# Moving the SBUF tiles of an attention and two-MoE kernel to multiples of 512 bytes

## The chip, the cores and the metric

The kernel runs on one NeuronCore of a Trainium2 chip, in one launch. The metric is device time in microseconds (us). Before the change, three runs gave a median of 1016.65 us (1014.98 to 1017.88). Lower is better.

## What is computed

Causal attention with a decay bias on 4 batches, 8 heads, 576 positions and head size 64, then two feed-forward stages on the 2304 tokens of width 512. All inputs and outputs are float32. The reference, cut to what matters:

```
scores = q @ k.T / sqrt(64)
cum    = cumsum(maximum(s, 0));  bias = minimum(-(cum[i] - cum[j]), 0)
attn   = softmax(where(causal, -1e9, scores + bias));  x = attn @ v   # -> [2304, 512]
x      = ((x @ w_a) * (x @ w_b)) @ w_out            # d_ff 1536
h      = x @ w_in                                    # d_ff 2048
out    = (maximum(h,0) + alpha*minimum(h,0)) @ w_out2
```

## The kernel before, in words

**Blocks.** The 2304 tokens are cut into four blocks of 512 and one of 256 (`blocks`). For each block `ffn(blk)` runs both feed-forward stages, and while it does, the attention steps of the next block are put between its matmuls (`steps`). Before the first block, `first_attention` does what block 0 needs.

**Float32 by three passes.** A float32 product is made of three matmuls on float32r operands. Each operand is split into a rounded part and a rest: x into `xh` and `xl`, a weight tile into `wh` and `wl` (`parts`), an activation g into `gh` and `gl` (`split_g`). `mm3` (lines 1076 to 1080) then issues three matmuls, L1077 to L1079; the second GEMM of the second stage issues its own three, L1188 to L1190:

```
nc.tensor.matmul(o, wh, ih, start=first, stop=False)   # L1077
nc.tensor.matmul(o, wh, il, start=False, stop=False)   # L1078
nc.tensor.matmul(o, wl, ih, start=False, stop=last)    # L1079
```

The second argument is the stationary operand (128 columns, loaded into the array before each matmul), the third the moving one, streamed past it: 512 columns in blocks 0 to 3, 256 in block 4. In the trace a matmul is written `bank<-moving,stationary`, so `bank<-xh,wh` streams `xh`, and `bank<-wh,gh` (L1188) streams `wh`, always 512 columns.

**Steps of a block.** Stage one has 12 steps (1536/128). A step is two times `into` (4 slices of x, three matmuls each: 24 that stream x) and four slices of the way back (12 that stream `gh` or `gl`). Stage two has 16 steps (2048/128). A step is one `into` (12 that stream x) and the way back, 12 matmuls that stream `wh` or `wl` (6 in the last block).

**Weights.** In block 0 each weight tile comes from `w64` as 64-bit words into a `raw` tile (`first`, a DMA on SP's queue), is decoded by ACT and DVE into `w32`, split into `wh` and `wl`, and also stored to DRAM (`store`, a DMA on ACT's queue, `w_d<-w`). In blocks 1 to 4 pairs of tiles come back from there into the same `raw` tiles (`load_pair`).

**Order.** The planner class `Order` fixes, from estimated durations, the order of all instructions while the kernel is built; at run time each engine works through its list and waits on semaphores.

**Where tiles lie.** Each tile pool takes one stretch of SBUF, one after the other in the order in which the pools are opened (lines 224 to 233). An address here is the byte within each partition. Before the change `alpha_sb` (64 bytes) stands among the constants, so that everything behind it starts at 64 modulo 512; the five `raw` tiles (4104 bytes, laid at steps of 4128) stand ahead of the weights and activations, so that these start at 480 modulo 512.

Of the kernel before, what the change touches and what calls it, by code (L numbers as in the profile page):

```python
# [9 lines left out]
F32 = mybir.dt.float32  # L10
F32R = mybir.dt.float32r
I32 = mybir.dt.int32
# [9 lines left out]
P = 128  # L22
# [26 lines left out]
def f32(ap):  # L49
    return ap.bitcast(F32)  # L50
# [148 lines left out]
def attention_two_moe_kernel(  # L199
# [15 lines left out]
    NF2 = alpha.shape[1]  # L215
    NW = w64.shape[0]
    NF1 = (NW - 2 * NF2) // 3
    WN = 512
# [5 lines left out]
    const = ctx.enter_context(tc.tile_pool(name="const", bufs=1))  # L224
    xp = ctx.enter_context(tc.tile_pool(name="xp", bufs=1))
    dram = ctx.enter_context(tc.tile_pool(name="dram", bufs=1, space=DRAM))
    raw = ctx.enter_context(tc.tile_pool(name="raw", bufs=1))
    work = ctx.enter_context(tc.tile_pool(name="work", bufs=1))
    small = ctx.enter_context(tc.tile_pool(name="small", bufs=12))
    wraw = ctx.enter_context(tc.tile_pool(name="wraw", bufs=1))  # L230
    wsp = ctx.enter_context(tc.tile_pool(name="wsp", bufs=6))
    gp = ctx.enter_context(tc.tile_pool(name="gp", bufs=3))
    ft = ctx.enter_context(tc.tile_pool(name="ft", bufs=4))
    ps = ctx.enter_context(tc.tile_pool(name="ps", bufs=1, space=PSUM))
    W32, RAW, KQ, VB, CB, KL, TOPS = 4, 5, 3, 4, 3, 2, 2
    ZT = 3
# [55 lines left out]
    def dma(o, i):  # L292
        yield {"sp": 480}, 700
        nc.sync.dma_start(o, i)
        yield {"dma": prod(o.shape) / (180 if o.dtype == U16 else 90)}, 900

    def split(src, hi, lo, sbuf=True):
        yield from copy(hi, src, 0.52 if sbuf else 1.04)
        yield from sub(lo, src, f32(hi), sbuf)
# [9 lines left out]

    ident = const.tile([P, P], F32, name="ident")  # L310
    make_identity(nc, ident)
    alpha_sb = const.tile([P, NF2], F32, name="alpha_sb")

    banks = [ps.tile([P, 512], F32, name=f"bank{i}") for i in range(8)]
    ab, acc = banks[2:4], banks[4:8]
# [665 lines left out]
    def decode(n, r, w):  # L981

        top = tops[n % TOPS]
        yield of_top
        yield {"act": 90 + 1.2 * WN}, SEEN
        nc.scalar.activation(
            top.bitcast(F16).rearrange("p (n t) -> p n t", t=2)[:, :, 1],
            r.bitcast(BF16)[:, 4:4 + 4 * WN].rearrange("p (n t) -> p n t", t=4)[:, :, 0],
            AF.Copy, scale=0.5,
        )  # L990
        rest = r[:, 0:2 * WN].rearrange("p (n t) -> p n t", t=2)[:, :, 1]
        yield from dve(
            WN, 1.04, nc.vector.scalar_tensor_tensor, w, rest, 13, top,
            op0=ALU.logical_shift_right, op1=ALU.bitwise_or, port=True
        )
        run.give(of_top, run.t)

    def load_pair(i):
        yield of_raw
        r = wraw.tile([P, 2 * WN + 2], F32, name="raw", tag="raw", bufs=RAW)  # L1000
        w = r[:, 0:2 * WN].rearrange("p (c n) -> p c n", c=2)
        pairs[i, "w"] = w
        yield from dma(w, w_d[i:i + 2].rearrange("c p n -> p c n"))

    def load_w(n):

        i = n % NW
        got = []

        def acquire():  # L1010

            if n:
                yield turns[n - 1]
            yield fetched
            yield of_w

        def first():
            yield of_raw
            r = wraw.tile([P, 2 * WN + 2], I32, name="raw", tag="raw", bufs=RAW)
            yield from dma(r.bitcast(U16)[:, 1:1 + 4 * WN], w64[i].bitcast(U16))  # L1020
            yield of_w32
            w = wraw.tile([P, WN], I32, name="w32", tag="w32", bufs=W32)
            if n == NW - 1:
                for j in range(2):
                    run.give(of_stack, run.t)
            source.append(w)
            yield from decode(n, r, w)
            run.give(of_raw, run.t)

        def again():  # L1030
            if i % 2 == 0:
                pairs[i] = run.spawn(load_pair(i))
            yield pairs[i - i % 2]
            source.append(pairs[i - i % 2, "w"][:, i % 2, :])

        def parts():
            yield turns[n]
            h = wsp.tile([P, WN], F32R, name="wh", tag="wh")
            l = wsp.tile([P, WN], F32R, name="wl", tag="wl")
            got.extend((h, l))  # L1040
            yield from split(f32(source[0]) if n < NW else source[0], h, l)
            if n < NW:
                run.spawn(keep(stored), run.t)
            elif i % 2:
                run.give(of_raw, run.t)

        def store():
            yield fetched
            yield {"act": 330}, 700
            nc.scalar.dma_start(w_d[i].bitcast(I32), source[0])  # L1050
            yield {"dma": P * WN / 90}, 900

        def keep(stored):
            yield stored
            run.give(of_w32, run.t)

        source = []
        fetched = run.spawn(first() if n < NW else again(), slack=SL_LOAD)
        stored = run.spawn(store()) if n < NW else None
        turns[n] = run.spawn(acquire())  # L1060
        return got, run.spawn(parts(), slack=SL_PARTS)
# [227 lines left out]
```

## Time and profile before

| | |
|---|---|
| median of three runs | 1016.65 us |
| profiled execution | 1019.79 us, span from first to last instruction 1018.0 us |
| mean granted TensorE clock | 0.995 |
| TensorE (PE) busy | 997.0 us, 98% of the span |
| VectorE (DVE), ScalarE (ACT), GpSimd (POOL) busy | 683.3, 554.9 and 241.6 us |
| DMA | 208.85 MB, mean 205 GB/s |

The profile covers one execution. Its timeline gives the start of each instruction. A matmul's duration in it is modelled, about 0.4 us for 512 columns, and overlaps the next one's, so the rate of TensorE is read from start to start: the time from one matmul's start to the next one's. The view by stretches counts the instructions that touch a stretch, gives the granted clock there, and the share of time for which the 16 DMA engines moved packets.

### The profile page before, as it was taken

To read this page: it belongs to the slowest core of one execution; us is meant where nothing else is said; L and a number is where in the kernel's file an instruction comes from. 1 tells how busy PE (TensorE), PEld (TensorE's weight loads), DVE (VectorE), ACT (ScalarE), POOL (GpSimd) and SP (SyncE) were. 2 spreads that over 40 slices of the span, in tenths; PEclk is the share of its full clock that TensorE was granted. 3 is DMA by queue.
4 is the path that set the end of the run, shared out by engine and by line. 5 is a ranking of instruction groups with operands and counts; after the bars stand their busy time and mean duration, and the time that the engine had idled before them with its cause. 6 is when DMAs were issued, how large, how long until landed. Compare 5 with 4: busy or idle time off the path is not lost.

```text
span 1018.0 us, 16223 instructions
## 1 busy us (share of the span) xinstructions
PE 997.0 (98%) x5381; PEld 810.5 (80%) x5381; DVE 683.3 (67%) x1590; ACT 554.9 (55%) x1133; POOL 241.6 (24%) x307
## 2 busy tenths in 40 slices
PE   6999999998999999999999999999999999999998
PEld 5667777776888888788888888888888888889997
DVE  6887767895578676866478677954444465546685
ACT  5865656775565455655454446544433354446574
POOL 2121112321232243433133124422010022220032
PEclk9999999998999999999999999999999999999999
DMA  6699999999677858458287656554542424317551
GB/s 164 206 282 347 354 329 335 322 335 308 231 258 220 243 167 257 144 166 259 83 265 238 201 201 181 179 176 129 182 144 88 156 86 135 109 63 248 181 174 60
DMA packets 149156, 208.85 MB, mean 205 GB/s; under 512 B 36112, under 2 KB 80144, under 8 KB 149072
## 3 DMA queue, kind: packets, MB, share of 16 engines
q1 hardware_dynamic: 139280, 189.99, 59.5%
q10 hardware_dynamic: 9792, 17.83, 4.7%
q8 instruction: 42, 0.69, 0.3%
q14 instruction: 42, 0.34, 0.1%
HBM read 164.18 MB, written 43.59 MB: 204 GB/s over the span
## 4 chain that ended last, share of the span: by engine, by line
PE 92%; DMA 4%; DVE 3%; ACT 0%; issue 0%; SPq 0%; POOL 0%; ACTq 0%; DVEq 0%; POOLq 0%
PE bank L1077 21%; PE bank L1078 21%; PE bank L1079 21%; PE bank L1188 6%; PE bank L1189 6%; PE bank L1190 6%; PE bank L765 3%; PE bank L501 2%; PE bank L527 2%; DMA cb<-cum_d 2%; PE bank L705 1%; PE bank L826 1%; DMA raw<-in_w_dram 1%; DVE z L277 1%; DMA kq<-in_kq_a_dram 1%; PE bank L517 1%
## 5 line engine op out<-in xcount | busy, mean ns | idle before, releaser
L1077 PE MATMUL bank<-xh,wh 128*128 128x512 f32 (+1 forms) x800 | 301.5, 377 | 2.1 <-DVE g L277 2.1
L1079 PE MATMUL bank<-xh,wl 128*128 128x512 f32 (+1 forms) x800 | 299.2, 374 | 0.0
L1078 PE MATMUL bank<-xl,wh 128*128 128x512 f32 (+1 forms) x800 | 298.5, 373 | 0.0
L269 ACT ACTIVATE wh<-raw 128x512 fp32r<-128x512 f32 x268 | 167.6, 628 | 102.5 <-PE bank L1078 60.6
L283 DVE TENSOR_TENSOR wl<-raw,wh 128x512 fp32r<-128x512 f32 x188 | 130.8, 698 | 100.3 <-ACT wh L269 94.5
L283 POOL TENSOR_TENSOR wl<-raw,wh 128x512 fp32r<-128x512 f32 x84 | 110.0, 1310 | 342.9 <-ACT wh L269 329.4
L1077 PEld LDWEIGHTS bank<-xh,wh 128*128 128x128 f32 x800 | 150.8, 189 | 35.8 <-issue 4.6
L1079 PEld LDWEIGHTS bank<-xh,wl 128*128 128x128 f32 x800 | 150.4, 188 | 28.9
L1078 PEld LDWEIGHTS bank<-xl,wh 128*128 128x128 f32 x800 | 150.3, 188 | 28.8
L269 ACT ACTIVATE gh<-g 128x512 fp32r<-128x512 f32 (+1 forms) x140 | 82.3, 588 | 70.7 <-DVE g L277 67.9
L1188 PE MATMUL bank<-wh,gh 128*128 128x512 f32 x288 | 115.2, 400 | 2.9 <-ACT wh L269 2.9
L283 DVE TENSOR_TENSOR gl<-g,gh 128x512 fp32r<-128x512 f32 (+1 forms) x128 | 87.9, 687 | 42.0 <-ACT gh L269 40.2
L1189 PE MATMUL bank<-wl,gh 128*128 128x512 f32 x288 | 114.3, 397 | 0.0
L1190 PE MATMUL bank<-wh,gl 128*128 128x512 f32 x288 | 113.3, 394 | 0.0
L261 ACT ACTIVATE z<-z,mn 128x128 f32<-128x128 f32 (+4 forms) x144 | 82.9, 577 | 52.8 <-DVE mn L277 52.8
L1077 PE MATMUL bank<-gh,wh 128*128 128x512 f32 (+1 forms) x240 | 90.1, 375 | 0.0
L1078 PE MATMUL bank<-gl,wh 128*128 128x512 f32 (+1 forms) x240 | 89.4, 372 | 0.2 <-DVE gl L283 0.2
L1079 PE MATMUL bank<-gh,wl 128*128 128x512 f32 (+1 forms) x240 | 88.7, 370 | 0.0
L261 ACT ACTIVATE m<-bank 128x512 f32<-128x512 f32 (+1 forms) x80 | 44.2, 553 | 81.1 <-PE bank L1079 80.7
L288 DVE TENSOR_SCALAR m<-m,alpha_sb 128x512 f32<-128x512 f32 (+1 forms) x68 | 33.2, 489 | 63.2 <-ACT m L261 62.2
L269 ACT ACTIVATE a_sb<-bank 128x512 f32<-128x512 f32 (+1 forms) x60 | 33.0, 550 | 66.5 <-PE bank L1079 64.0
L1188 PEld LDWEIGHTS bank<-wh,gh 128*128 128x128 f32 x288 | 54.6, 189 | 17.1 <-ACT wh L269 3.4
(91 smaller groups left out, 1369.6 us busy)
## 6 DMA issues: line engine op xcount, KB each, us to landing
raw<-w_d SPq DMA_DIRECT2D x136, 512.0 KB, 4.1
raw<-in_w_dram SPq DMA_DIRECT2D x68, 512.0 KB, 6.1
w_d<-w ACTq DMA_DIRECT2D x68, 256.0 KB, 5.6
zd<-zt SPq DMA_DIRECT2D x48, 192.0 KB, 4.1
pt<-zd SPq DMA_DIRECT2D x48, 192.0 KB, 4.0
kq<-in_kq_a_dram SPq DMA_DIRECT2D x16, 512.0 KB, 5.1
vb<-in_v_dram SPq DMA_DIRECT2D x112, 64.0 KB, 4.0
zd<-zt SPq DMA_DIRECT2D x24, 256.0 KB, 2.7
```

What stands on the lines that cost most here:

```text
L261: nc.scalar.activation(o, i, func, **k)
L269: nc.scalar.activation(o, i, AF.Copy, scale=by)
L283: (nc.gpsimd if eng == "pool" else nc.vector).tensor_tensor(o, i0, i1, op=ALU.subtract)
L288: (nc.gpsimd if eng == "pool" else nc.vector).tensor_scalar(o, i, s0, s1, op0=ALU.mult, op1=ALU.mult)
L501: nc.tensor.matmul(d, qs[:, r * P:n], k[:, 0:n], start=i == 0, stop=i == 1)
L765: nc.tensor.matmul(pv[64 * j:64 * j + 64, r * P:(r + 1) * P], got[0][:, c, j * D:(j + 1) * D], p[:, :, r * (r + 1) // 2 + c, :], start=c = ...
L1077: nc.tensor.matmul(o, wh, ih, start=first, stop=False)
L1078: nc.tensor.matmul(o, wh, il, start=False, stop=False)
L1079: nc.tensor.matmul(o, wl, ih, start=False, stop=last)
L1188: nc.tensor.matmul(acc[t], gh[:, c], wh, start=first, stop=False)
L1189: nc.tensor.matmul(acc[t], gh[:, c], wl, start=False, stop=False)
L1190: nc.tensor.matmul(acc[t], gl[:, c], wh, start=False, stop=last)
```

## The change

Two pools move. `small` (the minima and sums of the softmax, 32 bytes apart) goes behind the large tiles and also takes `alpha_sb`; the `raw` tiles leave the pool `wraw` for a new pool `w64p`, the last one.

```
-    small = ctx.enter_context(tc.tile_pool(name="small", bufs=12))
     wraw = ctx.enter_context(tc.tile_pool(name="wraw", bufs=1))
     wsp = ctx.enter_context(tc.tile_pool(name="wsp", bufs=6))
     gp = ctx.enter_context(tc.tile_pool(name="gp", bufs=3))
     ft = ctx.enter_context(tc.tile_pool(name="ft", bufs=4))
+    small = ctx.enter_context(tc.tile_pool(name="small", bufs=12))
+    w64p = ctx.enter_context(tc.tile_pool(name="w64p", bufs=1))
...
-    alpha_sb = const.tile([P, NF2], F32, name="alpha_sb")
+    alpha_sb = small.tile([P, NF2], F32, name="alpha_sb", bufs=1)
...
-        r = wraw.tile([P, 2 * WN + 2], F32, name="raw", tag="raw", bufs=RAW)
+        r = w64p.tile([P, 2 * WN + 2], F32, name="raw", tag="raw", bufs=RAW)
...
-            r = wraw.tile([P, 2 * WN + 2], I32, name="raw", tag="raw", bufs=RAW)
+            r = w64p.tile([P, 2 * WN + 2], I32, name="raw", tag="raw", bufs=RAW)
```

In the built programs every engine has the same instructions in the same order, with the same waits; only the addresses differ:

| tile | first address before (modulo 512) | after (modulo 512) |
|---|---|---|
| `xh`, `xl`: 4 slices of 2048 bytes each | 20544 (64) | 20480 (0) |
| `pt`, `kq`, `vb`, `z`, `zt`, `kl` | 59456 for the first (64) | 59392 (0) |
| `cb1`, second buffer | 108864 (320) | 108800 (256) |
| `w32`, also `kh` and `qs` | 176096 (480) | 154624 (0) |
| `wh`, `wl` | 184288 (480) | 162816 (0) |
| `gh`, `gl` | 208864 (480) | 187392 (0) |
| `a_sb`, `m`, `g`, `o` | 221152 (480) | 199680 (0) |
| the five `raw` tiles | 155456 (320, 352, 384, 416, 448) | 208704 (320, 352, 384, 416, 448) |

The `raw` tiles keep their places modulo 512, one by one.

## Rows read from the trace of the kernel before

**Rows 1.** Page, part 1: engine, busy us, share of the span, instructions.

```profile
PE 997.0 (98%) x5381; PEld 810.5 (80%) x5381; DVE 683.3 (67%) x1590; ACT 554.9 (55%) x1133; POOL 241.6 (24%) x307
```

**Rows 2.** Page, part 4: the chain that ended last, by engine and by line.

```profile
PE 92%; DMA 4%; DVE 3%; ACT 0%; issue 0%; SPq 0%; POOL 0%; ACTq 0%; DVEq 0%; POOLq 0%
PE bank L1077 21%; PE bank L1078 21%; PE bank L1079 21%; PE bank L1188 6%; PE bank L1189 6%; PE bank L1190 6%; PE bank L765 3%; PE bank L501 2%; PE bank L527 2%; DMA cb<-cum_d 2%; PE bank L705 1%; PE bank L826 1%; DMA raw<-in_w_dram 1%; DVE z L277 1%; DMA kq<-in_kq_a_dram 1%; PE bank L517 1%
```

**Rows 3.** Waits of TensorE: total us, times, longest; first and last of nine.

```profile
PE bank L366 <- DVE cum L355: 5.7, 1, 5.7
...
PE bank L1078 <- DVE gl L283: 0.2, 1, 0.2
```

**Rows 4.** TensorE groups by line and shape: count, busy us, mean ns.

```profile
L1077 PE MATMUL bank<-xh,wh 128*128 128x512 f32 x640 | 256.4, 401 | 2.1 <-DVE g L277 2.1
...
L1188 PE MATMUL bank<-wh,gh 128*128 128x512 f32 x288 | 115.2, 400 | 2.9 <-ACT wh L269 2.9
...
L1077 PE MATMUL bank<-gh,wh 128*128 128x512 f32 x192 | 76.5, 399 | 0.0
```

**Rows 5.** Timeline of TensorE, x streaming: start us, modelled us, instruction.

```profile
737.16 0.39 PE L1077 MATMUL bank<-xh,wh 128*128 128x512 f32 x1
737.39 0.39 PE L1078 MATMUL bank<-xl,wh 128*128 128x512 f32 x1
737.62 0.40 PE L1079 MATMUL bank<-xh,wl 128*128 128x512 f32 x1
737.86 0.39 PE L1077 MATMUL bank<-xh,wh 128*128 128x512 f32 x1
```

**Rows 6.** Timeline of TensorE, wh and wl streaming.

```profile
717.63 0.39 PE L1188 MATMUL bank<-wh,gh 128*128 128x512 f32 x1
717.85 0.39 PE L1189 MATMUL bank<-wl,gh 128*128 128x512 f32 x1
718.08 0.39 PE L1190 MATMUL bank<-wh,gl 128*128 128x512 f32 x1
718.31 0.39 PE L1188 MATMUL bank<-wh,gh 128*128 128x512 f32 x1
```

**Rows 7.** Stretches, TensorE alone: us, busy (instructions touched), clock, DMA share, GB/s.

```profile
733.64:742.01 8.37, 8.37 (x37) 1.00 0.43 140
694.41:699.98 5.57, 5.57 (x25) 1.00 0.33 97
...
954.12:957.00 2.88, 2.88 (x26) 1.00 0.73 194
```

**Rows 8.** Timeline of TensorE, L521, which streams one repeated column.

```profile
29.39 0.33 PE L521 MATMUL bank<-rows,cums 64*128 64x384 f32 x2
29.55 0.48 PE L527 MATMUL bank<-kq 64*128 64x384 f32 x2
...
30.43 0.38 PE L521 MATMUL bank<-rows,cums 64*128 64x512 f32 x2
30.65 1.02 PE L527 MATMUL bank<-kq 64*128 64x512 f32 x4
```

**Rows 9.** Timeline of TensorE in a stretch of half clock.

```profile
250.43 0.63 PE L1188 MATMUL bank<-wh,gh 128*128 128x512 f32 x1
...
251.71 0.63 PE L1188 MATMUL bank<-wh,gh 128*128 128x512 f32 x1
```

**Rows 10.** Stretches, all engines: PE, PEld, DVE, ACT, POOL; clock, DMA share, GB/s.

```profile
50.00:250.00 200.00, 194.93 (x1025) 149.42 (x1025) 151.25 (x361) 128.23 (x255) 42.03 (x55) 0.99 1.00 327
250.00:490.00 240.00, 237.88 (x1268) 193.77 (x1267) 172.10 (x393) 129.25 (x267) 75.83 (x96) 0.99 0.69 214
```

**Rows 11.** ScalarE groups by line and shape: count, busy us, mean ns.

```profile
L269 ACT ACTIVATE wh<-raw 128x512 fp32r<-128x512 f32 x268 | 167.6, 628 | 102.5 <-PE bank L1078 60.6 <-PE bank L1190 17.1 <-issue 16.7
...
L269 ACT ACTIVATE kh<-kq 128x512 fp32r<-128x512 f32 x16 | 9.3, 619 | 3.9 <-DMA kq<-in_kq_a_dram 2.0 <-PE bank L501 1.9
```

**Rows 12.** DMA queue of ACT (w_d<-w): packets, MB, share of 16 engines.

```profile
q10 hardware_dynamic: 9792, 17.83, 4.7%
```

## Prediction

> **What bounds the kernel now.** I read the page's busy times first: TensorE is busy for 997.0 of 1018.0 us [rows 1]. The chain of waits says the same, 92% of it TensorE, and two thirds of that the three lines of `mm3` [rows 2]. TensorE's nine waits start at 5.7 us for the longest and end at 0.2; two thirds of what they sum to lies before block 0 [rows 3]. So nothing is gained here by ending a wait sooner, only by a matmul that takes less, and a layout can change only that: no instruction, no order and no wait differs.
>
> How long a matmul takes is read from start to start. Three matmuls that stream x follow each other in 737.86 - 737.16 = 0.70 us, 233 ns each [rows 5]; three that stream `wh` and `wl` in 718.31 - 717.63 = 0.68 us, 227 ns each [rows 6]. 512 columns at 2.4 GHz are 213.3 ns, so there are 13 to 20 ns in every matmul that are no column. Three more rows say what they are not. At the low clock, 1.2 GHz, three of the same matmuls start in 1.28 us, 427 ns each, which is 512 columns and nothing else [rows 9]: a fixed price for changing the stationary operand would be there too. L521 is also float32r and also changes its stationary operand each time, but it streams one column over and over, so that hardly anything is fetched; the next line starts 0.22 us after it for 512 columns and 0.16 for 384 [rows 8], which, at the 10 ns that these rows resolve, is the columns and a few ns at most. And the two kinds with the extra time differ from each other: x lies at 64 modulo 512 and takes 233, `wh` at 480 and takes 227. All three point to the fetch of the moving operand from SBUF at the high clock, and to its address.
>
> The sizes fit a simple picture. 227 ns are 544 column times, and 544 = 17 x 32: a run of 2048 bytes that starts between multiples of 128 bytes touches 17 pieces of 128 bytes, where 16 would hold it. In block 4, 24 matmuls of 256 columns take 2.88 us, 120 ns each [rows 7], or 288 column times = 9 x 32, where 8 pieces would do. If the fetch runs at just the rate of the columns, one piece per 32 columns, the piece too many is what the extra time is. That is argued from sums, not shown; no operand at a multiple of 128 bytes is streamed at this rate in the trace.
>
> **The change part by part.** What TensorE spends in the two feed-forward stages, from rows: a step of stage one is 24 + 12 matmuls in 8.37 us, a step of stage two 12 + 12 in 5.57 us [rows 7]. Four blocks of 12 and 16 steps make 4 x (12 x 8.37 + 16 x 5.57) = 758 us. Block 4 adds 12 x 36 x 0.120 + 16 x (12 x 0.120 + 6 x 0.23) = 97 us. Together 855 us, 84% of the span, in 3 x (640 + 192 + 288) = 3360 matmuls of 512 columns [rows 4] and 624 of 256.
>
> Moving x, weights and activations to 0 modulo 512. The trace shows no such operand, so the price is bounded from both sides. Lower end: the start to start of L521, taken as the columns and 2.5 ns, since 0.22 and 0.16 both allow that: 216 ns for 512 columns and 109 for 256. The steps become 36 x 0.216 = 7.78 and 24 x 0.216 = 5.18 us, the four blocks 4 x (12 x 7.78 + 16 x 5.18) = 705 us, block 4 12 x 36 x 0.109 + 16 x (12 x 0.109 + 6 x 0.216) = 89 us: 61 us less. Upper end: all at the 233 ns of rows 5, steps of 8.40 and 5.60 us, 4 us more. I take the lower end, because the two sizes of the extra time are each just one 128-byte piece, and because the stationary and the moving operand then have the same place modulo 512, as only the 227 ns kind has now.
>
> Block 0 won't give all of its share. Its quarter of the 53 us that the four blocks save is 13 us, but from 50 to 250 us the 16 DMA engines are busy for 1.00 of the time at 327 GB/s [rows 10], with the weights coming in and going out. What TensorE saves there it will mostly wait for the next weight tile. I keep 3 of 13 us: 10 less saved. After block 0 the share is 0.69, DVE is busy for 172 of 240 us and ACT for 129 [rows 10]; a pace 6% faster leaves both under 80%. For waits that are hidden now and come out there (splits of g, transposed probabilities) I take off 2 us; none to 10 is the range.
>
> Everything else is about nothing. ACT's copies of 512 columns take 628 ns from `raw` tiles and 619 from `kq`, which lie at five and at one place modulo 512 [rows 11]; so an ACT instruction may change by 2% at most, 11 us of ACT's 555, hidden behind TensorE; without that cover it would be these 11 us. The `raw` loads keep their places modulo 512. The stores `w_d<-w` now start at a multiple of 512; they are 4.7% of the DMA engines' time, 48 us, in block 0 [rows 12], and a tenth either way would be 5 us there, in the stage that the DMAs set. I take nothing and keep 5 us each way for the range.
>
> Sum: -61 + 10 + 2 = -49 us. On the profiled execution (span 1018.0 us and 1.8 around it, 1019.8) that is 971; it ran 3 us above the median of the three runs, 1016.65, on which I forecast 1016.65 - 49 = **968 us**.
>
> **Rivals.** *Only the worse of the two places is mended.* The 13 ns are a start-up of the fetch, not a piece too many, and only the 6 ns between x and `wh` go, with the 50 ns by which a step of stage one, 8.37 us, is longer than 24 x 0.2333 + 12 x 0.2267 = 8.32. Then all run at 226.7: steps of 8.16 and 5.44 us, 4 x (12 x 0.21 + 16 x 0.13) = 18 us less, of which block 0 gives back 3: 1001 us. For it: the extra is 13 ns for 256 columns and for 512 alike, as a start-up would be. Against it: L521 and the half clock show none.
>
> *The layout doesn't matter.* x differs from `wh` and `gh` also in its PSUM banks (2 and 3 against 4 to 7) and in where in SBUF it lies; if one of these makes the 6 ns, the time stays 1017 us. For it: no row holds all else equal. Against it: L521 also ends in a bank and has no extra. [...]
>
> *Slower: the same start for everything collides.* Moving and stationary operand are both fetched, and now begin at the same place modulo 512, on a multiple of 64 as x does already; x at 64 is the slower kind, `wh` at 480 the faster. If a start on such a multiple is what costs, x stays at 233 and the 1440 matmuls that stream weights and activations go from about 230 ns ((8.37 - 24 x 0.2335)/12) to 233: with the steps of 8.40 and 5.60 us above, 4 x (12 x 0.03 + 16 x 0.03) and as much per matmul in block 4, 3.7 us more, 1020 us. It decides the sign if these 1440 lose 2 ns or more each, 3 us, while x stays.
>
> **How the numbers follow.** Fetch without the extra piece, 968: 0.43. Only the worse place mended, 1001: 0.25. Between these two (a part of the extra, 975 to 998): 0.06. No effect, 1017: 0.13. Slower, 1020 and up: 0.13. A measurement of this kernel tells about 0.3% (3 us) from no change. Faster is then 0.43 + 0.25 + 0.06 = 0.74, the same 0.13, slower 0.13. The likeliest case's own range is 955 (all 61 us) to 980 (10 more us of new waits, DMAs 2 worse). The range of 8 in 10 has to hold both faster cases and about half of no effect: 955 to 1017.
>
> **What would show it.** In the profile after, a step of stage one should take 7.8 us instead of 8.37 and one of stage two 5.2 instead of 5.57, at clock 1.00; x and weights should have the same start to start, 216 ns, and block 4's 256 columns 109. TensorE's busy share should fall in block 0 alone, with waits on `wh` or `wl` and the DMA share still near 1.00; ACT's 628 ns should stay. If steps take 8.16 and 5.44 the first rival is right; if x keeps 233 ns, the address is not what sets it and the forecast is wrong.

## The result and the profile after

The changed kernel took 1005.9 us (median of 4 runs, 1001.92 to 1007.81) against 1017.26 us for the kernel before beside it (4 runs): ratio 0.9881, 95% interval 0.9841 to 0.9921. So it is faster by 11 us, 1.2%, not by the 49 us forecast. The profiled execution has a span of 1006.0 us. Its source lines stand one higher than before (L1078 for L1077).

The pace of the matmuls first. The timeline of TensorE in the changed kernel, x streaming (two more matmuls stand between these lines):

```profile
713.16 0.39 PE L1078 MATMUL bank<-xh,wh 128*128 128x512 f32 x1
...
713.84 0.39 PE L1078 MATMUL bank<-xh,wh 128*128 128x512 f32 x1
```

Three matmuls now take 0.68 us where [rows 5] have 0.70: 227 ns each, the pace that `wh` and `wl` had in [rows 6], and no less. Steps of stage one and two, and 24 matmuls of block 4, TensorE alone (us, busy and instructions touched, clock, DMA share, GB/s):

```profile
717.24:725.40 8.16, 8.16 (x37) 6.76 (x36) 4.66 (x7) 3.65 (x7) 0.00 (x0) 1.00 0.83 269
711.80:717.24 5.44, 5.44 (x25) 4.50 (x24) 1.64 (x3) 2.38 (x6) 0.68 (x3) 1.00 0.95 304
...
942.11:944.99 2.88, 2.88 (x26) 2.88 (x25) 1.32 (x4) 1.53 (x3) 0.00 (x0) 1.00 0.79 195
```

(These rows list PE, PEld, DVE, ACT and POOL.) Against [rows 7], a step of stage one went from 8.37 to 8.16 us, one of stage two from 5.57 to 5.44, and block 4's 256 columns stayed at 120 ns. Both steps are now exactly 226.7 ns per matmul, 36 and 24 of them. So at clock 1.00 a column more costs (226.7 - 120.0)/256 = 0.417 ns, or 1/2.4, and 512 of them 213.3; at the half clock of [rows 9] it is 427/512 = 0.834 ns. These 2.4 and 1.2 columns per ns are what the forecast writes as GHz. Before, the matmuls behind those that stream x were slowed too: the 12 of the way back, whose operands both lie at 480, took 230 ns each there and take 226.7 now.

```profile
739.26:742.01 2.76, 2.76 (x13) 1.00 0.58 190
```

The same five blocks of work, before and after, from each block's first feed-forward matmul to the next one's. Before:

```profile
57.02:285.20 228.18, 224.24 (x1174) 0.99 0.95 311
285.20:503.63 218.43, 216.31 (x1137) 1.00 0.65 199
503.63:719.67 216.04, 216.04 (x1138) 1.00 0.61 192
719.67:916.73 197.06, 197.06 (x913) 1.00 0.39 124
916.73:1013.90 97.17, 97.00 (x720) 1.00 0.51 167
```

After:

```profile
56.00:283.50 227.50, 220.82 (x1175) 0.98 0.93 312
283.50:499.80 216.30, 213.98 (x1137) 0.99 0.64 201
499.80:711.80 212.00, 212.00 (x1137) 1.00 0.62 196
711.80:904.70 192.90, 192.90 (x914) 1.00 0.39 127
904.70:1001.90 97.20, 97.03 (x720) 1.00 0.52 167
```

Blocks 2 and 3, in which TensorE never waits, are 4.0 and 4.2 us shorter. Block 1 is 2.1 shorter, block 0 0.7, block 4 the same. In block 0 TensorE is busy for 3.4 us less and the block is hardly shorter: it waits 6.7 us there instead of 3.9, of which one wait for a `wh` tile is 4.6 instead of 2.9. ACT's copies from `raw` take 626 ns, where [rows 11] have 628.

The granted clock has a part in this. Around that wait for `wh`, TensorE ran at half the clock (0.50 in the rows below) for 6.8 us in both kernels; in block 1 it did so for 3.4 us in the changed one alone, behind a wait of 2.3 us. The first row is the kernel before, the others are the changed one:

```profile
247.64:254.47 6.83, 5.85 (x13) 0.50 0.98 331
246.12:252.95 6.83, 5.39 (x12) 0.50 0.79 260
413.38:416.79 3.41, 3.41 (x10) 0.50 0.75 221
```

At half the clock a matmul of 512 columns takes 427 ns [rows 9] instead of 227, so by an estimate from these two the 3.4 us cost block 1 1.6 us; without them it would have gained 3.7.

So the gain is a faster pace of matmul in blocks 0 to 3, and the question is on what address it depends, and why it stops at 226.7 ns.

### The profile page after: what moved, and what is told of

It reads as the page before. It is cut to its first block, busy times and chain, and to the rows that moved or that the text cites. A ratio compares the mean times of both kernels' runs of the same rounds, so it can differ in the third digit from the quotient of the medians.

```text
span 1006.0 us, 16223 instructions
## 1 busy us (share of the span) xinstructions
PE 982.2 (98%) x5381; PEld 810.7 (81%) x5381; DVE 682.8 (68%) x1590; ACT 553.5 (55%) x1133; POOL 243.2 (24%) x307
## 4 chain that ended last, share of the span: by engine, by line
PE 86%; DMA 7%; DVE 3%; issue 1%; ACT 1%; POOL 1%; ACTq 0%; SPq 0%; POOLq 0%; DVEq 0%
PE bank L1078 20%; PE bank L1079 20%; PE bank L1080 19%; PE bank L1189 6%; PE bank L1190 6%; PE bank L1191 6%; PE bank L766 2%; DMA cb<-cum_d 2%; PE bank L502 2%; DMA raw<-in_w_dram 2%; PE bank L528 1%; PE bank L706 1%; DMA kq<-in_kq_b_dram 1%; PE bank L827 1%; DVE z L278 1%
## 5 line engine op out<-in xcount | busy, mean ns | idle before, releaser
L1078 PE MATMUL bank<-xh,wh 128*128 128x512 f32 (+1 forms) x800 | 299.1, 374 | 2.3 <-DVE g L278 2.3
L1079 PE MATMUL bank<-xl,wh 128*128 128x512 f32 (+1 forms) x800 | 295.1, 369 | 0.0
L1080 PE MATMUL bank<-xh,wl 128*128 128x512 f32 (+1 forms) x800 | 295.1, 369 | 0.0
L1078 PEld LDWEIGHTS bank<-xh,wh 128*128 128x128 f32 x800 | 151.0, 189 | 33.2 <-issue 4.1
L1078 PE MATMUL bank<-gh,wh 128*128 128x512 f32 (+1 forms) x240 | 89.9, 374 | 1.1 <-ACT wh L270 1.1
```

## The experiments

In what follows "64/480" means: the moving operand starts 64 bytes, the stationary one 480 bytes behind a multiple of 512.

### pace: TensorE alone, a stretch of 36 matmuls per layout

One line per stretch, for instance (m and s take the bytes, b cycles through the kernel's 8 `bank` tiles):

```
for i in range(36):
    mm(b(i), s(480, i), m(64), start=True, stop=True)
```

> This kernel leaves out the whole computation: TensorE alone runs stretches of 36 matmuls, 128x128 stationary, 512 float32r columns moving, one stretch for each start of the moving operand (0, 32, 64, 96, 128, 192, 256, 320, 384, 448, 480 bytes behind a multiple of 512) and of the stationary one, then a repeated column as moving operand, bf16 operands, 128 to 384 columns, 64 stationary columns, 64 rows, one stationary operand throughout, one bank throughout. Theory A (start-up of each float32r matmul, whatever the address): 226.7 ns from start to start with both at 0, near 216 for the repeated column and for bf16, n/2.4 + 13 ns for fewer columns. On the address, theory A1 (the distance between the two operands modulo 512 makes the other 6.7 ns): 226.7 wherever both are at the same place (32/32, 64/64, 480/480), 233 at 64/480 and at most unequal places. Theory A2 (the moving operand's own place makes it): the same pace for a given moving place whatever the stationary one, 233 at 64, 227 at 0 and 480. Theory B (the forecast's, a piece of 128 bytes too many): some place of the moving operand at a multiple of 128 gives 216; if both at 0 gives 226.7 again, B has fallen.

Measured: the middle 30 matmuls of a stretch from start to start, in the order 0/0, 64/0, 128/0, 256/0, 0/64, 64/64, 480/480, 64/480, then a repeated column, bf16, and 192 and 384 columns at 0/0; at last 64 rows, one stationary operand throughout, one PSUM bank throughout. Stretches, TensorE alone (the last row is a start of 64/64):

```profile
20.86:27.66 6.80, 6.80 (x32) 1.00 0.01 2
37.44:44.30 6.86, 6.86 (x31) 1.00 0.00 0
54.11:61.11 7.00, 7.00 (x31) 1.00 0.00 0
70.90:77.70 6.80, 6.80 (x32) 1.00 0.00 0
120.89:127.89 7.00, 7.00 (x31) 1.00 0.00 0
170.89:177.70 6.81, 6.81 (x32) 1.00 0.01 2
179.09:185.91 6.82, 6.82 (x31) 1.00 0.00 0
187.30:194.31 7.01, 7.01 (x32) 1.00 0.00 0
195.64:202.20 6.56, 6.56 (x31) 1.00 0.01 2
203.52:209.99 6.47, 6.47 (x31) 1.00 0.00 0
214.87:218.22 3.35, 3.35 (x32) 1.00 0.00 0
223.48:228.68 5.20, 5.20 (x32) 1.00 0.00 0
238.43:245.24 6.81, 6.81 (x32) 1.00 0.01 2
246.81:253.62 6.81, 6.81 (x32) 1.00 0.00 0
263.14:269.94 6.80, 6.80 (x32) 1.00 0.00 0
...
169.97:171.58 1.61, 1.61 (x9) 1.00 0.05 10
```

Divided by 30: 226.7 ns (6.80 us) at 0/0, at 256/0 and, but for a few matmuls of transition, at 64/64 and 480/480; 233 (7.00) at 128/0, 0/64 and 64/480, the kernel's own layout before; 229 (6.86) at 64/0. The transition is the first seven matmuls behind a stretch of another layout: at 64/64 they took 1.61 us, 230 ns each. Theory A2 falls: with the moving operand at 0, the stationary one's place alone makes 226.7 or 233. Theory A1 holds, with two things that it had not: a distance of 256 is as good as 0, and 64/0 costs only 2 ns. Theory B, the forecast's, falls: both operands at a multiple of 512 still take 226.7. The repeated column takes 219 (6.56 us) and bf16 216 (6.47); 384 columns take 173.3 (5.20), again 13.3 more than their 160 at 1/2.4 ns each. Of the rest of A, rows, banks and a stationary operand that never changes make no difference (6.81, 6.80 and 6.81 us). Its n/2.4 + 13 ns fails for few columns: 192 take 111.7 ns, where it has 93, and 128 take about as long, by an estimate: their 36 lie between the end of the bf16 stretch at 210.24 us and the first of 192 columns, four matmuls ahead of its row, at 214.42, so 116 ns each.

### all64 and x0w160: the change in two halves

all64 is the changed kernel with `alpha_sb` left among the constants:

```
-    alpha_sb = small.tile([P, NF2], F32, name="alpha_sb", bufs=1)
+    alpha_sb = const.tile([P, NF2], F32, name="alpha_sb")
```

> The change without its alpha_sb edit: x, weights and activations all at 64 modulo 512, so moving and stationary operand still start at the same place. Theory A1 (distance between the operands): as the full change, 227 ns for x and for the others, a step of stage one 8.16 us, about 1006 us, ratio to before 0.988. Theory A2 (place of the moving operand): all at 233, steps of 8.40 and 5.60 us, about 1020 us, ratio 1.004.

x0w160 is the changed kernel with the `raw` tiles back in their old pool (one of its two lines):

```
-        r = w64p.tile([P, 2 * WN + 2], F32, name="raw", tag="raw", bufs=RAW)
+        r = wraw.tile([P, 2 * WN + 2], F32, name="raw", tag="raw", bufs=RAW)
```

> The change without the move of the raw tiles: x at 0, weights and activations at 160 modulo 512. Theory A1 (distance): the matmuls that stream x, with stationary weights at 160, stay slow at about 233 ns, those that stream g or weights (both operands at 160) take 227; steps near 8.37 and 5.57 us, about 1016 us, ratio 1.00. Theory A2 (place of the moving operand): x gains its 6.7 ns, 1920 matmuls, 12 us less if the others at 160 are as those at 480; about 1005 us, ratio 0.988.

Measured: all64 1005.83 us, ratio 0.9904 (0.9879 to 0.9930); x0w160 1016.03 us, ratio 1.0011 (0.9989 to 1.0034). A step of each stage, TensorE alone, in all64:

```profile
711.24:719.40 8.16, 8.16 (x38) 1.00 0.86 272
705.80:711.24 5.44, 5.44 (x26) 1.00 0.96 299
```

and in x0w160:

```profile
721.60:729.96 8.36, 8.36 (x38) 1.00 0.81 263
866.78:872.32 5.54, 5.54 (x25) 1.00 0.24 67
```

With everything at 64 the steps are those of the full change; with x at 0 but weights at 160 they are, within 0.03 us, those of before. Both came out as A1 has it and against A2. So it isn't the multiple of 512 that pays, it is that x and the weights start at the same place, and moving `alpha_sb` brings nothing that these runs can tell.

### pace2: what the remaining 13 ns are not

The same stretches with other operands, for instance a stationary operand of one column repeated:

```
mm(b(i), st[:, 0:1].to_broadcast([P, 128]), m(0), start=True, stop=True)
```

> Again TensorE alone, the computation left out. Stretches of 36 matmuls with fewer stationary columns (128, 64, 32, 16, 8), with one stationary column repeated 128 times (so that its load fetches hardly anything) at three starts of the moving operand, with finer and farther starts, with float32r runs of 256 to 448 columns at a distance of 96 bytes, and bf16 at 0 and 96 bytes. Theory A (start-up of the moving operand's own fetch): with the repeated stationary column still 226.7 ns. Theory C (the load of the next stationary operand and the stream of the moving one meet in SBUF): with the repeated stationary column near 216 ns at all three starts, and a pace that doesn't depend on the start; with few stationary columns also toward 216. On the distance, the period is 256 bytes: 228.8 at 64 whichever operand is shifted (64/0 and 0/192), 233 at 160 and 224. For bf16 A and C both allow 216 at 0; at 96 C expects more if it is the meeting and not the rate that counts, A 216.

Measured, again 30 matmuls each: 64 and 16 stationary columns at 0/0; the repeated stationary column with the moving operand at 0 and at 96; 64/0 and 0/192; then 96/0 with 256, 320, 384 and 448 columns; a moving operand that takes every other column; 4/0; at last 15 matmuls of bf16 at 96/0.

```profile
29.66:36.55 6.89, 6.89 (x31) 1.00 0.00 0
46.28:53.23 6.95, 6.95 (x31) 1.00 0.00 0
62.94:69.89 6.95, 6.95 (x31) 1.00 0.00 0
79.62:86.57 6.95, 6.95 (x31) 1.00 0.01 2
121.40:128.27 6.87, 6.87 (x32) 1.00 0.00 0
154.79:161.66 6.87, 6.87 (x31) 1.00 0.00 0
171.00:174.60 3.60, 3.60 (x32) 1.00 0.02 5
175.43:179.83 4.40, 4.40 (x32) 1.00 0.00 0
180.84:186.14 5.30, 5.30 (x32) 1.00 0.00 0
187.31:193.47 6.16, 6.16 (x31) 1.00 0.01 3
...
211.21:224.76 13.55, 13.55 (x32) 1.00 0.00 0
96.16:103.26 7.10, 7.10 (x31) 1.00 0.00 0
204.90:208.14 3.24, 3.24 (x15) 1.00 0.00 0
```

Theory C falls as stated: with the stationary column repeated the pace is 232 ns (6.95 us for 30), not 216, and that at both starts. Theory A misses here too: it had 226.7 for the repeated column. To repeat the stationary column doesn't take the 13 ns away; with 128 different columns at 0/0 it even goes faster, 226.7. That the pace with the repeated column doesn't depend on the start (6.95 us at 0 and at 96) does fit C's meeting of the two streams, which no run shows. 64/0 and 0/192 both take 229 (6.87 us): a distance of -192 is as one of 64, so the period is 256 bytes here too. The starts of 80, 160 and 224 bytes together, between the stretches of 64/0 and 0/192, took 25.15 us (128.73 to 153.88) for 108 matmuls, 233 ns each, as expected for 160 and 224, and 4/0 the most, 237 (7.10 us for 30). At 96/0, the distance of x and weights in the kernel before, 256 columns take 120.0, 320 take 146.7, 384 take 176.7 and 448 take 205.3: above n/2.4 these are 13, 13, 17 and 19 ns, and 20 for 512 (8.41 us for 36, in pace). That is why block 4, with its 256 columns, gained nothing. 512 columns taken as every other one of 1024 take 452 ns (13.55 us for 30), twice the 226.7. bf16 took 216 ns at 96 (3.24 us for 15) as at 0 (6.47 for 30, in pace), as A has it.

What the 13 ns are is left open: a contiguous float32r moving operand took at least 13 ns above n/2.4 in every row here. They stay with a repeated stationary column (18 ns), and at 0/0 they don't change with one stationary operand throughout, one bank, 64 rows (6.81, 6.80 and 6.81 us for 30 in pace) or, from 256 to 512 columns (120.0, 173.3 and 226.7 ns), the length. A stretch without the weight load was not shown: the kernel before has 5381 loads for 5381 matmuls [rows 1], and `wh` is loaded for L1077 and again for L1078.

### rawonly and full_again: one edit against the whole

rawonly is the kernel before, with the `raw` tiles alone moved to the end; `small` and `alpha_sb` stay (one of the two lines with `raw`):

```
     ft = ctx.enter_context(tc.tile_pool(name="ft", bufs=4))
+    w64p = ctx.enter_context(tc.tile_pool(name="w64p", bufs=1))
...
-        r = wraw.tile([P, 2 * WN + 2], F32, name="raw", tag="raw", bufs=RAW)
+        r = w64p.tile([P, 2 * WN + 2], F32, name="raw", tag="raw", bufs=RAW)
```

> The move of the raw tiles alone, on the kernel before: small and alpha_sb stay where they were, so x lies at 64 and weights and activations at 320 modulo 512, 256 bytes apart and neither at a multiple of 128. If equal places modulo 256 are what counts: 227 ns everywhere, ratio as for the full change, 0.985 to 0.993. If equal places modulo 512 or multiples of 128 are needed: x stays at 233 and the ratio is near 1.00.

> The full change beside the move of the raw tiles alone, on the same chip. Equal places modulo 256 count: the two agree within 0.3%, both about 1.1% below the kernel before. Otherwise the full change is about 1% faster than the move alone.

Measured on one chip: rawonly 1002.53 us, ratio 0.9836 (0.9804 to 0.9869); the full change again 1003.23 us, ratio 0.9848 (0.9819 to 0.9878). In rawonly:

```profile
714.37:722.53 8.16, 8.16 (x37) 1.00 0.95 270
708.93:714.37 5.44, 5.44 (x25) 1.00 0.91 298
```

With x at 64 and the weights at 320, neither a multiple of 128, the steps are 8.16 and 5.44 us: a period of 256, not 512, and the move of the `raw` tiles alone does all that the change does. None of the versions beats the full change by more than its interval. In the second profile of the full change block 0 and 1 are shorter than in the first:

```profile
57.00:278.10 221.10, 217.96 (x1175) 1.00 0.95 322
278.10:492.80 214.70, 212.38 (x1137) 1.00 0.66 202
...
244.29:251.12 6.83, 6.52 (x27) 1.00 0.97 311
406.59:410.00 3.41, 3.41 (x15) 1.00 0.64 210
```

Block 0 takes 221.1 us against 227.5 for the same work; blocks 2 to 4 agree within 0.1 us. Of these 6.4 us, 3.5 are waits (3.1 against 6.7) and 2.9 are in TensorE's busy time. The last two rows show why: they start at the wait for `wh`, 1.8 us here, and behind the wait of 2.3 us in block 1, and TensorE keeps its full clock in both, where the first profile has 0.50. With that block 1 is 1.6 us shorter as well. So what block 0 gives back differs from one execution to the next, in the wait for a weight tile and in the clock behind it; the same wait of 2.3 us in block 1 was followed by half the clock in one execution and not in the other.

## Why the prediction was wrong

**The bound was read rightly.** TensorE's pace sets the time, the order and the other engines don't change with the layout, ACT's durations stayed (626 ns for 628), and the gain is read where it was said to be, in the length of a step.

**The step that failed is "I take the lower end".** The term was 61 us, from steps of 7.78 and 5.18 us at 216 ns; the steps measured 8.16 and 5.44. The 216 ns were taken from L521, which streams a repeated column [rows 8]. pace has that operand alone: 219 ns, and 226.7 for a contiguous one at 0/0. The 2.5 ns that the forecast puts on the columns were its author's estimate, within the 10 ns that the row resolves; no run shows them for float32r, where the repeated column took 5.4 ns above its 213.3 and the contiguous one 13.3. That hardly anything is fetched for the repeated column was the author's reading as well; no run shows what is fetched. The row was right for what it showed, a repeated column, and said nothing of 512 different ones; it was an end of the range and no more. The kernel had a hint of the other value: for the float32r matmuls of the attention its planner counts n / 2.4 + 13 ns each (L504). With 226.7 in the sum instead of 216, the term is 4 x (12 x 0.21 + 16 x 0.13) = 18 us. Measured, blocks 2 and 3 gave 4.0 and 4.2 us each of the 4.6 that this has for a block, since other steps of before took 8.36 and 5.55 us. That 1005.9 still lies between 955 and 1017 is owed to the first rival, for which that range was made wide, and not to the mechanism of the forecast.

**The picture behind it was wrong.** 544 = 17 x 32 and 288 = 9 x 32 fitted a 128-byte piece too many to the column. But operands that start at a multiple of 512 need no such piece and take the same 544 and 288. n + 32 columns fits the same two numbers, and was the first rival's "start-up", with its argument written beside it: the extra is the same for 256 and 512 columns.

**The first rival was the case.** It gave steps of 8.16 and 5.44 us, to the digit, and 1001 us; measured were 1005.9 and, the second time, 1003.2. It had a chance of 0.25. Its mechanism was half right: an extra of 13 ns that stays was shown (13.3 at 0/0), that it is a start-up of the fetch was not, and that "the worse of two places" is mended is wrong. There are no good and bad places, only distances: x at 64 is fast when the weights are at 64 (all64) or 320 (rawonly), and slow when they are at 480. The 50 ns that it adds to a step of stage one are for the most part the 12 matmuls behind x, 2.76 us before and 2.72 at 226.7 ns each.

**No effect, and slower.** A difference between the kinds of matmul by bank or region is ruled out by pace, in which one pair of tiles gives 226.7 and 233 by distance alone. The collision of equal starts is ruled out by 0/0: equal starts are the fast case, 226.7 ns. And that the layout doesn't matter is ruled out by 64/64 and 64/480, which differ by 7 ns.

**Block 0 and the rest.** In block 0 the faster pace saved 3.4 us of TensorE's busy time. In the first profile the block gave 0.7 of them, the rest went into longer waits for weights, as the forecast had it for most of its 13 us; in the second the waits were shorter than before and the block gave 7.1, of which about 3, by an estimate from 427 and 227 ns for a dozen matmuls, are the half clock that the kernel before had there. So the term "10 less saved" was of the right kind, and how much is held back isn't settled. What the forecast didn't weigh is the clock behind a wait. Stalls that come out in the later blocks, 2 us in the sum, were not seen: in blocks 2 and 3 TensorE is busy throughout, and in block 1 it waits 2.3 us instead of 2.1.

## What to carry to other kernels

A row that shows the best pace of another kind of operand bounds a gain, but doesn't forecast it; the best pace of the same kind (227 ns here, [rows 6]) is the value to take. Where float32r matmuls of 384 columns or more follow each other with full clock, lay the moving and the stationary operand so that their starts agree modulo 256 bytes (226.7 ns for 233 at 512 columns here, 173.3 for 176.7 at 384); tiles of odd sizes go to the end of SBUF. Before an edit of a layout, a stretch of 36 matmuls per address on TensorE alone tells what it can bring. And before two profiles are compared block by block, compare the granted clock in the blocks: 1.6 us of block 1 were clock and not layout.

## What the runs showed of the hardware

The start of the moving operand against that of the stationary one decided the pace of float32r matmuls at clock 1.00: 226.7 ns for 512 columns at a distance of 0 or 256 bytes (6.80 us for 30), 229 at 64 (6.86), 233 at 32, 96, 128 and 192 (8.40 or 8.41 us for the 36 of a stretch), 237 at 4 (7.10 for 30). At 256 columns a distance of 96 cost nothing (120.0 ns at 96/0 in pace2 and at 0/0 in block 4), and at 320 the 146.7 ns are the same 13 above n/2.4. The place of the stationary operand alone, 0/0 against 0/64, makes 7 ns of 227 (6.80 and 7.00 us for 30). The bf16 matmuls of pace took 215.7 ns (6.47 us for 30), 2.4 above 512 columns at 1/2.4 ns. A contiguous float32r operand at 0/0 took 13.3 ns more than its columns, at 256, 384 and 512 alike (120.0, 173.3 and 226.7).
